# The first load of a decode kernel, issued as 16 rows and then 112

## The chip, the cores and the metric

The kernel runs on one core of a Trainium2 chip. The metric is the device time of one execution in microseconds; lower is better. The core's engines are TensorE (PE, whose weight loads are shown as PEld), VectorE (DVE), ScalarE (ACT), GpSimd (POOL) and SyncE (SP), which here issues nearly all transfers. Transfers run on 16 DMA engines beside them.

## The reference

One token is decoded. The input x (1 x 1 x 512) is layer-normalised; an attention block with 32 heads of 128 reads a cache of 8192 keys and values for each head; a gated linear unit makes a gate; the result is x + s · silu(g). All numbers are float32.

```python
xn = _layernorm(x, axis=-1)
# attention: q = (xn @ wq) in 32 heads of 128
scores = jnp.einsum("bhqd,bhkd->bhqk", q, k_cache) * (Dh ** -0.5)
p = _softmax(scores, axis=-1)
o = jnp.einsum("bhqk,bhkd->bhqd", p, v_cache)
s = o.transpose(0, 2, 1, 3).reshape(B, Sq, H * Dh) @ wo
# gate
h = _sigmoid(xn @ w_gate) * (xn @ w_up)
g = _silu(h @ w_down)
out = x + s * g
```

The key and value caches are 128 MiB (134 MB) each; wq and wo are 8 MiB each, and w_gate, w_up and w_down about 2.7 MiB each. Every byte is read once.

## The kernel before, in words

SBUF holds three large buffers, `slots[0]` to `slots[2]`, each 64 KB in each of 128 partitions. Heads are worked in 16 pairs. The keys of a pair fill one of the slots 0 and 1 by turns (two heads, 64 partitions each, 128 positions of 128 floats in a partition), the values of a pair fill slot 2. VectorE multiplies the keys with the query in place (L415) and sums over the head's 128 numbers (L416); TensorE and ScalarE do the maximum, the powers and the product with the values. At the end wo is loaded into a free slot in nine pieces (L484) and multiplied by VectorE and TensorE together.

Before the first pair the slots serve the small weights. wq lies in slot 2 as four blocks of 4096 columns (partition p holds rows 4p to 4p + 3 of wq) and is loaded in two halves, blocks 0 and 1 and then blocks 2 and 3; both are called by `load_queries` (L191). w_gate and w_up go to slot 0, the first pair's keys to slot 1. All of these go out on SyncE's queue, in the program's order: the first half of wq (L194) ahead of the branch into the compiled part (L196, where the engines meet), and the rest behind it. Only the input row x is loaded on ScalarE's queue (L240). w_down follows in slot 2, as a body of 128 rows and a remainder of 32 rows that go to every fourth partition (L321 and L324).

`load` (L163) is the helper behind every such transfer: it takes a name, gives that name a semaphore when it is new, adds 16 to the count to be waited for, issues the transfer and returns semaphore and count. A transfer that is waited for has landed when its semaphore has reached the count. VectorE waits for the first half of wq in the loop at L294 and starts `in_place` (L286), which scales wq's blocks by the normalised x (L289) and adds them up (L290, L307).

From the second pair on SyncE issues each load when its slot is free again: a key slot when VectorE has summed it, the value slot when TensorE has used it. A load therefore stands in the queue well before its turn on the DMA engines comes.

Of the kernel before, what the change touches and what calls it, by code (L numbers as in the profile page):

```python
# [13 lines left out]
P = 128  # L14
# [37 lines left out]
def kernel(  # L52
# [44 lines left out]
    DVE, ACT, SP, POOL = nc.vector, nc.scalar, nc.sync, nc.gpsimd  # L97
# [49 lines left out]
    def semaphore(name):  # L147
        return unused.pop(0)
# [14 lines left out]
    def load(eng, name, dst, src, *after):  # L163
        wait(eng, *after)
        if name not in loads:
            loads[name] = [semaphore(f"s_{name}"), 0]
        loads[name][1] += 16
        ins = eng.dma_start(dst, src)  # L168
        if not tc.compiled:
            tc.no_tile_sem_insts.add(ins.ins.name)  # L170
        ins.then_inc(loads[name][0], 16)
        return loads[name][0], loads[name][1]

    def wait(eng, *steps):
        for s in steps:
            if s is not None:
                eng.wait_ge(*s)
# [10 lines left out]
    xv = x.rearrange("a b d -> (a b d)")  # L188
    wq_t = slots[2].rearrange("p (k c) -> p k c", k=KT)
    wq_v = wq.rearrange("(p k) c -> p k c", k=KT)  # L190
    def load_queries(n):  # L191
        return load(SP, f"wq{n}", wq_t[:, n:n + 2, :], wq_v[:, n:n + 2, :])

    ld_wq = [load_queries(0)]  # L194
    tc.close()
    tc.compile()  # L196
    ld_wq.append(load_queries(2))
    wg_t, wu_t = (slots[0][:, n * KT * F:(n + 1) * KT * F].rearrange("p (k f) -> p k f", f=F) for n in range(2))
    ld_g = load(SP, "wg", wg_t, w_gate.rearrange("(p k) f -> p k f", k=KT))
# [157 lines left out]
    n = FL // NG  # L357
# [149 lines left out]
    for k, r in enumerate(W_DVE):  # L507
        n = k % 2
# [90 lines left out]
```

## Time and profile before

| | |
|---|---|
| median of three runs | 684.52 us (684.47 to 685.29) |
| the profiled execution | 684.89 us |
| its span, first to last instruction | 683.4 us |
| VectorE busy | 615.2 us (90%) |
| TensorE matmuls busy | 216.2 us (32%) |
| ScalarE busy | 44.6 us (7%) |
| mean granted TensorE clock | 0.668 |
| bytes read | 293.67 MB |

The page of a profile gives busy times of each engine over the span, then the span cut into 40 equal slices: a digit is the busy share in tenths, and a row of GB/s says what the DMA engines moved. Instructions are grouped by line, engine and operation, `out<-in` with the program's names for tensors and slots; "SPq" is the sequencer of SyncE, which issues transfers. A stretch of the run, given by its start and end in microseconds from the span's start, can be asked for by itself. For a transfer the page gives its size and the time from issue to landing. A packet counts with all its bytes at its start in such tables, so the GB/s of a stretch of a microsecond or two are rough.

### The profile page before, as it was taken

The numbers are of one execution on the slowest core, as the hardware profiler recorded it, in microseconds if no ns is written. First come the engines' busy times: TensorE is split into PE (matmuls) and PEld (weight loads), VectorE is DVE, ScalarE is ACT, GpSimd is POOL, SyncE is SP. The second block draws the span as 40 slices with busy tenths as digits, with TensorE's granted clock in tenths as the row PEclk, the third lists the DMA queues.
The fourth block names the chain that finished last, engine by engine and source line by source line (L and its number), as shares of the span: only waits on it lengthen the run. The fifth ranks groups of instructions, "written<-read, shape, count | busy, mean of one in ns | idle before, by whom it ended". The sixth has DMA issues, their size and how long they took to land. (4 is left out here: it accounts for less than half of the span.)

```text
span 683.4 us, 3400 instructions
## 1 busy us (share of the span) xinstructions
PE 216.2 (32%) x1376; PEld 62.0 (9%) x1376; DVE 615.2 (90%) x156; ACT 44.6 (7%) x142; POOL 2.6 (0%) x11
## 2 busy tenths in 40 slices
PE   0353024060513206050412406050422406060666
PEld 0120001010100101010100101010100101010110
DVE  3879999999999998998989899898989999999917
ACT  2130010000000101000000100000010101000010
POOL 0000000000000000000000000000000000000000
PEclk9996657575665757575665757575665757575886
DMA  9999999999999999999999999999999999999998
GB/s 382 429 440 472 430 430 430 430 430 430 430 430 430 430 430 430 430 456 456 437 430 430 430 430 430 430 430 430 430 430 445 449 441 399 476 399 430 430 430 337
DMA packets 7552, 293.67 MB, mean 430 GB/s; under 512 B 856, under 2 KB 864, under 8 KB 1664
## 3 DMA queue, kind: packets, MB, share of 16 engines
q1 hardware_dynamic: 7544, 293.67, 99.5%
q10 hardware_dynamic: 8, 0.00, 0.0%
HBM read 293.67 MB, written 0.00 MB: 430 GB/s over the span
## 5 line engine op out<-in xcount | busy, mean ns | idle before, releaser
L415 DVE TENSOR_TENSOR slot<-slot,q_all 128x16384 f32<-128x16384 f32 (+3 forms) x19 | 275.9, 14522 | 21.4 <-DMA slot<-in_A_k_cache_dram 21.4
L416 DVE TENSOR_REDUCE sc<-slot 128x128 f32<-128x16384 f32 (+3 forms) x19 | 276.0, 14525 | 0.7
L38 PE MATMUL psum<-slot,zeros 128*8 128x512 f32 x1024 | 145.5, 727 | 261.5 <-PEq L38 261.5
L38 PEld LDWEIGHTS psum<-slot,zeros 128*8 128x8 f32 x1024 | 30.2, 102 | 363.3 <-issue 363.3
L38 PE MATMUL psum<-ident,mx 128*1 128x128 f32 x32 | 8.7, 372 | 108.6 <-PEq L38 108.6
L437 ACT COPY o<-psum 128x512 f32<-128x512 f32 x16 | 9.4, 586 | 405.1 <-PE psum L38 405.1
L38 PE MATMUL psum<-slot,ones 128*128 (+3 forms) x36 | 15.9, 612 | 21.9 <-PEq L38 16.2
L290 DVE SCALAR_TENSOR_TENSOR slot<-slot,xn 128x1376 f32<-128x1376 f32 (+1 forms) x8 | 18.9, 2360 | 3.0 <-DMA slot<-in_A_wq_dram 2.7
L38 PE MATMUL psum<-o,pick 128*2 128x128 f32 x128 | 16.5, 272 | 12.8 <-PEq L38 12.8
L423 DVE STREAM_TRANSPOSE psum<-psum 32x128 f32<-32x128 f32 x16 | 5.0, 310 | 11.1 <-PE psum L38 11.1
L430 ACT ACTIVATE zeros<-sc,nb 64x128 f32<-64x128 f32 x32 | 12.8, 399 | 0.9
L38 PEld LDWEIGHTS psum<-o,pick 128*2 128x2 f32 x128 | 9.9, 84 | 29.6 <-issue 27.2
L428 ACT ACTIVATE nb<-psum 128x2 f32<-128x2 f32 x16 | 2.8, 172 | 150.9 <-PE psum L38 150.9
L38 PE MATMUL psum<-slot,o_all 128*1 128x128 f32 (+1 forms) x54 | 10.7, 510 | 5.3 <-DMA slot<-in_A_wo_dram 5.3
L38 PEld LDWEIGHTS psum<-ident,mx 128*1 128x1 f32 x32 | 1.9, 80 | 112.6 <-issue 112.6
L408 DVE TENSOR_REDUCE mx<-psum 1x2 f32<-1x128 f32 x16 | 4.4, 277 | 7.8 <-PE psum L38 7.8
L38 PE MATMUL psum<-zeros,rs 128*32 128x2 f32 x32 | 3.8, 188 | 23.5 <-PEq L38 23.5
L38 PE MATMUL psum<-mx,ones 1*128 1x2 f32 x32 | 8.4, 330 | 7.4 <-PEq L38 7.4
L515 DVE SCALAR_TENSOR_TENSOR q_all<-slot,o_all,q_all 128x512 f32<-128x512 f32 x15 | 10.0, 747 | 0.0
L38 PE MATMUL psum<-slot,o 128*1 128x512 f32 x26 | 5.5, 910 | 12.8 <-DMA slot<-in_B_w_down_dram 12.8
L38 PEld LDWEIGHTS psum<-slot,ones 128*128 128x128 f32 (+1 forms) x36 | 6.4, 201 | 31.3 <-issue 23.3
L38 PEld LDWEIGHTS psum<-mx,ones 1*128 1x128 f32 x32 | 7.5, 290 | 14.3 <-issue 14.3
(54 smaller groups left out, 60.5 us busy)
## 6 DMA issues: line engine op xcount, KB each, us to landing
slot<-in_A_k_cache_dram SPq DMA_DIRECT2D x2, 6144.0 KB, 37.9
slot<-in_A_v_cache_dram SPq DMA_DIRECT2D x3, 4096.0 KB, 22.7
slot<-in_A_wq_dram SPq DMA_DIRECT2D x2, 4096.0 KB, 16.3
slot<-in_A_k_cache_dram SPq DMA_DIRECT2D x2, 4096.0 KB, 40.5
slot<-in_A_k_cache_dram SPq DMA_DIRECT2D x2, 2048.0 KB, 42.4
slot<-in_B_w_gate_dram SPq DMA_DIRECT2D x1, 2752.0 KB, 26.7
slot<-in_B_w_up_dram SPq DMA_DIRECT2D x1, 2752.0 KB, 32.7
slot<-in_B_w_down_dram SPq DMA_DIRECT2D x1, 2560.0 KB, 24.1
```

The source lines that it names most:

```text
L38: ins = getattr(self.engine, name)(*args, **kwargs)
L290: return dve(DVE.scalar_tensor_tensor(y, w[:, k, cols], xn[:, k:k + 1], y, op0=ALU.mult, op1=ALU.add))
L408: DVE.reduce_max(mx[:1, 1:3], pt[0:1, :].rearrange("o (e p) -> o e p", e=2), axis=AX.X).then_inc(reduced, 1)
L415: wait(DVE, dve(DVE.tensor_mul(k[:, j, :], k[:, j, :], qb[:, i:i + 1, :].to_broadcast([P, n, Dh]))))
L416: summed[i] = dve(DVE.reduce_sum(sc[i % 2][:, j], k[:, j, :], axis=AX.X))
L423: turned_out[i] = dve(DVE.transpose(o, pn.rearrange("e (a r) -> e a r", r=WR)))
L428: wait(ACT, act(ACT.mul(nb, pm[:, :2], -SCALE)))
L430: ACT.activation(weights[h, :, e * HT:(e + 1) * HT], sc[i % 2][h].rearrange("p (g b) -> p g b", b=HT), AF.Exp, bias=nb[h, e:e + 1], scale= ...
L437: ACT.copy(o1, po).then_inc(copied, 1)
L515: ins = DVE.scalar_tensor_tensor(part[n], wo_t[:, r, :], col, part[n], op0=ALU.mult, op1=ALU.add)
```

## The change

`load_queries` takes partitions at which the load is cut, and issues one transfer for each run of partitions between cuts. The first half of wq is cut at partition 16: a transfer of 16 rows and one of 112 rows, each row 32 KB. Both have the same name, so they share one semaphore, and the count that is returned, and waited for by VectorE, is that of both. The second half is called without cuts and stays one transfer of 128 rows.

```diff
     wq_v = wq.rearrange("(p k) c -> p k c", k=KT)
-    def load_queries(n):
-        return load(SP, f"wq{n}", wq_t[:, n:n + 2, :], wq_v[:, n:n + 2, :])
-
-    ld_wq = [load_queries(0)]
+    def load_queries(n, *cuts):
+        for a, b in zip((0,) + cuts, cuts + (P,)):
+            ld = load(SP, f"wq{n}", wq_t[a:b, n:n + 2, :], wq_v[a:b, n:n + 2, :])
+        return ld
+
+    ld_wq = [load_queries(0, 16)]
     tc.close()
     tc.compile()
     ld_wq.append(load_queries(2))
```

## The prediction, made before the changed kernel was run

> **What bounds the kernel now.** I read the two strips of the page first, the 40 slices of DMA and of bandwidth, because a kernel that reads 293.67 MB once each should be judged by its stream of transfers.
>
> ```profile
> DMA  9999999999999999999999999999999999999998
> GB/s 382 429 440 472 430 430 430 430 430 430 430 430 430 430 430 430 430 456 456 437 430 430 430 430 430 430 430 430 430 430 445 449 441 399 476 399 430 430 430 337
> DMA packets 7552, 293.67 MB, mean 430 GB/s; under 512 B 856, under 2 KB 864, under 8 KB 1664
> q1 hardware_dynamic: 7544, 293.67, 99.5%
> ```
>
> The DMA engines are busy in every slice. Queue q1, SyncE's, holds 99.5% of sixteen engines' whole span, and only the first slice (382) and the last (337) fall clearly below 430 GB/s. To see how the ends differ from the middle I asked for four stretches of the run (columns: the stretch, its length, busy time and count of PE, PEld, DVE, ACT, POOL, the granted clock, DMA share, GB/s):
>
> ```profile
> 0.00:1.70 1.70, 0.00 (x0) 0.00 (x0) 0.00 (x0) 0.00 (x0) 0.21 (x4) 1.00 0.00 0
> 1.70:4.00 2.30, 0.00 (x0) 0.00 (x0) 0.17 (x1) 0.29 (x1) 0.97 (x6) 1.00 1.30 456
> 4.00:680.00 676.00, 215.27 (x1356) 61.62 (x1360) 614.48 (x153) 44.29 (x142) 1.38 (x1) 0.66 1.00 433
> 680.00:683.40 3.40, 0.97 (x24) 0.36 (x24) 0.58 (x2) 0.00 (x0) 0.00 (x0) 0.97 0.02 8
> ```
>
> Nothing moves before 1.70 us, the share is 1.00 for 676 us, and then there are 3.4 us of tail. So the time is start plus bytes over rate plus tail: whatever moves the start of the stream moves the end by as much, and whatever leaves engines at half speed for a moment is never made up, since no engine has a gap to catch up in. The chain of waits ends in the same stream:
>
> ```profile
> by line: DMA slot<-in_A_wo_dram 4.2%; PE psum L38 1.0%; SPq L168 0.4%; SPq L227 0.1%; issue 0.1%; DVE g_row L537 0.0%; DVE g_row L539 0.0%
> 650.71 28.58 DMA slot<-in_A_wo_dram
> ...
> 680.59 0.44 PE psum L38 x8
> ```
>
> The last transfer waited for is one of wo, landed shortly before 680.59; behind it come two small VectorE operations and the store.
>
> **The change part by part.** SyncE issues the first load in two pieces instead of one; the two add up to the same 4096 KB. The rows below are the first of SyncE's program, up to the branch into the body; slot is slot2 for the queries' weights, slots 0 and 1 for the gate, up and key loads. Before:
>
> ```order
> L594 UNCONDITIONAL_BRANCH
> L168 DMA slot<-in_A_wq_dram 128x8192
> L196 UNCONDITIONAL_BRANCH
> L168 DMA slot<-in_A_wq_dram 128x8192
> L168 DMA slot<-in_B_w_gate_dram 128x5504
> ```
>
> And with the change, at the same place of the same engine:
>
> ```order
> L596 UNCONDITIONAL_BRANCH
> L168 DMA slot<-in_A_wq_dram 16x8192
> L168 DMA slot<-in_A_wq_dram 112x8192
> L198 UNCONDITIONAL_BRANCH
> L168 DMA slot<-in_A_wq_dram 128x8192
> ```
>
> One 128-row issue became 16 and 112; all behind it, on this engine and on the four others, stands as it stood. These rows, of the DMA issues (size of one, median time to landing), of SyncE's timeline (start, length) and of its waits, price the issue and the start:
>
> ```profile
> slot<-in_A_wq_dram SPq DMA_DIRECT2D x2, 4096.0 KB, 16.3
> ...
> 0.74 0.38 SPq L168 DMA_DIRECT2D slot<-in_A_wq_dram  x1
> 1.91 0.33 SPq L168 DMA_DIRECT2D slot<-in_A_wq_dram  x1
> 36.85 0.33 SPq L168 DMA_DIRECT2D slot<-in_B_w_down_dram  x1
> 38.29 0.57 SPq L168 DMA_DIRECT2D slot<-in_B_w_down_dram  x1
> SPq L196 <- PEq L196: 0.4, 2, 0.3
> ```
>
> *The added issue.* It costs SyncE 0.33 to 0.57 us. SyncE waits for PE at L196 anyway, 0.3 us in its longest wait, so the start of the other engines and the second load slip by 0 to 0.3 us (0.57 − 0.3). That is hidden twice. In the queues, by the first load: 4096 KB at 430 GB/s are 9.8 us, and the second load is issued 1.2 us behind the first (1.91 − 0.74). On VectorE, by these rows:
>
> ```profile
> 12.53 0.23 DVE L279 TENSOR_SCALAR xn<-xc,st 128x4 f32<-128x4 f32 x1
> 12.90 2.35 DVE L289 TENSOR_SCALAR slot<-slot,xn 128x4096 f32<-128x4096 f32 x1
> 15.29 4.49 DVE L290 SCALAR_TENSOR_TENSOR slot<-slot,xn 128x4096 f32<-128x4096 f32 x1
> 22.50 4.49 DVE L290 SCALAR_TENSOR_TENSOR slot<-slot,xn 128x4096 f32<-128x4096 f32 x1 [2.73 <-DMA slot<-in_A_wq_dram]
> ```
>
> Its work on wq begins at 12.90 and then idles 2.73 us for the second load. A start 0.3 us late is swallowed there. If that cover were gone, the price is the same 0.3 us, and still not on the end, because the stream doesn't wait for VectorE in those microseconds. Sum: 0.
>
> *The semaphore.* Both pieces raise the first load's semaphore, and VectorE waits for twice the count, so it still starts when all 128 rows are in. One more 4-byte packet for each engine, 16 beside 7552: 0.
>
> *The start of the stream.* This is the term that can be a gain. From the stretch 4 to 680, the rate is 433 GB/s, at which 293.67 MB take 678.2 us. They ended just before 680.59, so at full rate they would have started at about 2.3 us, 1.6 us after the issue at 0.74 (the rate's last digit is worth 0.8 us). A first piece with an eighth of the rows can win no more than those 1.6 us, and nothing if the delay doesn't hang on the rows. The row nearest to it says that fewer rows aren't quicker: w_down's 32-row remainder took 0.57 us to issue and its 128-row body 0.33. That is the issue, not the first byte, so a little may remain; I take an eighth of the bound, 0.2 us, and keep 0 to 1.6.
>
> *Which engine writes where.* In place of one load in which every engine has eight rows, each engine now has one row of partitions 0 to 15 and then seven of the others. A row of 8192 floats is 32 KB, and at a sixteenth of 430 GB/s it takes 1.22 us: a row-time below. Eight row-times for each engine before, 1 + 7 after, if rows run at full speed wherever they land. No load of the trace goes to 16 neighbouring partitions. The nearest is w_down's remainder, 32 rows in every fourth partition:
>
> ```profile
> slot<-in_B_w_down_dram SPq DMA_DIRECT2D x1, 2560.0 KB, 24.1
> slot<-in_B_w_down_dram SPq DMA_DIRECT2D x1, 192.0 KB, 23.1
> ```
>
> The body landed at 36.85 + 24.1 = 60.95, the remainder at 38.29 + 23.1 = 61.39: 0.44 us for 192 KB, which at 430 GB/s take 0.46. So a quarter of the partitions is written at the full rate, and I take 0 for this term. But those rows lie four apart, and 16 rows side by side can fare worse: bounds 0 and +12.2 us, worked out under the first rival.
>
> [...]
>
> **Sum.** The profiled execution took 684.89 us, span 683.4 and 1.49 around it; −0.2 gives 684.7. The median of the three runs is 684.52, 0.37 below the profiled one, and I forecast against it: **684.3 us**.
>
> **The rivals.** *Neighbours share a way in: slower.* If four neighbouring partitions are written through one path no faster than one engine, the 16-row piece keeps four paths busy for four row-times while the others wait: +3 row-times, 3.7 us. Then come sevens of consecutive rows for each engine, whose neighbours' rows share groups of four; at worst two engines meet all the time, and seven row-times become 14. Together 4 + 14 = 18 against 8, +10 row-times or 12.2 us; midway, 7 row-times, +8.5 us. Nothing is caught up afterwards, as the share is 1.00 to the end. It decides as soon as two engines want one group. 684.5 + 8.5 = **693.0**, from 688.2 to 696.7. For it: an engine's and a path's rates can't be told apart while each engine has partitions of its own. Against it: the remainder's 0.44 us. [...]
>
> *The 16 rows don't go one to each engine.* No view names the engine of a packet. If four engines took four rows each and the 112 rows still went seven to each, those four would have 11 rows: +3 row-times, 3.7 us, **688.2**. If the 112 rows evened that out, nothing changes, and it falls to the forecast.
>
> *The start wins all it can: faster.* −1.6 us, **682.9**, if the whole delay to the first bytes hangs on the number of rows. Against it: the 32-row issue that was no shorter.
>
> **How the numbers follow.** The forecast, no contention and a start between 0 and 1.6 us earlier, most of it within 0.2%: 0.51. Shared paths: 0.40, so high because the one row that speaks of it touches every group once. Uneven spread: 0.06. The full gain: 0.03. Two tenths of a per cent, 1.37 us, is about what a measurement of this kernel can tell from no change. So faster 0.03, same 0.51, slower 0.46 (0.40 + 0.06). The forecast's own range is 683.5 to 685.3. The range given must take in most of the shared paths: below 683.5 I leave out the full gain, 0.03, and above 694.0 the upper third of the first rival, 0.13. Range **683.5 to 694.0**.
>
> **What would show it.** If I am right, the slice strip begins as before, the stretch 1.70 to 4.00 holds some 450 GB/s or more, the last wo transfer lands within half a microsecond of 680.5, and VectorE's first operation on wq starts at about 12.9. If paths are shared, the stretch from 2 to 7 us shows a DMA share near 1 at far less than 430 GB/s (a packet in hand counts as busy), the first wq operation starts some 5 to 8 us late, and the last transfer lands later by the same 4 to 12 us with the middle of the run unchanged. If the spread is uneven, some engines go idle or run ahead and the share falls below 1. If the 16-row issue is longer than 0.57 us, the added-issue term is wrong. What would overturn all of it is a change in the middle: a lower rate from 20 to 680 us, which nothing in this edit explains.

## The result, and the profile after

The changed kernel took **694.77 us** (median of four runs, 694.35 to 695.01) against 684.84 us for the kernel before on the same chip: a ratio of 1.0141, with a 95% interval of 1.0129 to 1.0153. That is 9.9 us slower, where 684.3 us were forecast; the range ended at 694.0. Of the cases that the prediction named, the first rival came true and not the forecast.

The strips and the DMA queue of the page after:

```profile
DMA  9999999999999999999999999999999999999997
GB/s 212 381 458 413 468 423 431 423 423 454 446 427 427 423 431 469 423 431 423 423 450 450 427 427 423 427 469 427 427 427 433 429 448 407 460 420 423 421 420 312
DMA packets 7568, 293.67 MB, mean 423 GB/s; under 512 B 872, under 2 KB 880, under 8 KB 1680
q1 hardware_dynamic: 7560, 293.67, 99.3%
```

The DMA row still reads 9 everywhere, as before. Only the row below it tells the loss: 212 GB/s in the first slice, where 382 stood, then 381 in the second, where 429 stood. "Busy" counts an engine that holds a packet, however slowly the packet moves: in the stretch from 6 to 18 us below the share is still 0.90 at 235 GB/s, and in the eight blocks further down 1.02 at 119. The 16 packets more (7568 against 7552) are all under 512 B (872 against 856) and go with the added load: three loads added make 48 more (7600), seven 112 (7664).

Three stretches of the kernel before (columns as in the prediction; the last two are DMA share and GB/s):

```profile
6.00:18.00 12.00, 1.17 (x4) 1.00 (x4) 6.73 (x10) 1.42 (x2) 0.00 (x0) 1.00 0.99 429
6.00:34.00 28.00, 6.96 (x14) 3.65 (x15) 19.93 (x21) 4.18 (x10) 0.00 (x0) 1.00 1.00 433
60.00:640.00 580.00, 170.78 (x1164) 48.47 (x1164) 549.31 (x82) 29.91 (x107) 0.00 (x0) 0.63 1.00 434
```

and two of the same of the kernel after:

```profile
6.00:18.00 12.00, 1.18 (x4) 1.01 (x4) 1.66 (x8) 1.85 (x4) 0.00 (x0) 1.00 0.90 235
...
60.00:640.00 580.00, 168.37 (x1132) 47.49 (x1132) 551.05 (x94) 29.91 (x107) 0.00 (x0) 0.63 1.00 434
```

From 60 to 640 us nothing has changed, 434 GB/s in both. From 6 to 18 us the first half of wq comes in at 235 GB/s in place of 429. What was lost there stays lost, because the share is 1.00 from 60 to 640 us. The timeline of VectorE shows the loss arriving at its first work on wq, and the chain of waits shows it at the end:

```profile
16.44 0.23 DVE L281 TENSOR_SCALAR xn<-xc,st 128x4 f32<-128x4 f32 x1
22.63 2.35 DVE L291 TENSOR_SCALAR slot<-slot,xn 128x4096 f32<-128x4096 f32 x1 [5.96 <-DMA slot<-in_A_wq_dram]
```

```profile
660.02 30.02 DMA slot<-in_A_wo_dram
...
690.71 0.44 PE psum L38 x8
```

The first operation on wq starts at 22.63 instead of 12.90, 9.7 us late. The last wo transfer is used at 690.71 instead of 680.59, 10.1 us late. Nearly the whole of the loss is made in the first 22 us.

The kept traces also hold the start and the length of every packet, though no view lists them; one packet is one row of 32 KB of wq. The last of the first 128 rows ends at 21.56 us instead of 12.48, 9.1 us late. In the kernel before, the first 16 rows take 1.75 us on average and the others 1.22, 16 of them under way at a time. In the kernel after, the first 16 take 3.68 us and the 112 others 2.12, again 16 at a time.

### The profile page after: what moved, and what is told of

Same layout as the page of the kernel before. It is cut to its first block, busy times and chain, and to the rows that moved or that the text cites. A ratio compares the mean times of both kernels' runs of the same rounds, so it can differ in the third digit from the quotient of the medians.

```text
span 693.5 us, 3401 instructions
## 1 busy us (share of the span) xinstructions
PE 221.6 (32%) x1376; PEld 62.6 (9%) x1376; DVE 615.8 (89%) x156; ACT 44.6 (6%) x142; POOL 2.6 (0%) x11
## 2 busy tenths in 40 slices
DMA packets 7568, 293.67 MB, mean 423 GB/s; under 512 B 872, under 2 KB 880, under 8 KB 1680
## 5 line engine op out<-in xcount | busy, mean ns | idle before, releaser
L38 PE MATMUL psum<-slot,zeros 128*8 128x512 f32 x1024 | 149.8, 745 | 252.0 <-PEq L38 252.0
L38 PE MATMUL psum<-slot,ones 128*128 (+3 forms) x36 | 17.4, 657 | 27.4 <-PEq L38 22.0
L291 DVE TENSOR_SCALAR slot<-slot,xn 128x1376 f32<-128x1376 f32 (+1 forms) x3 | 4.8, 1595 | 6.0 <-DMA slot<-in_A_wq_dram 6.0
```

The lines of the kernel that those rows point to most:

```text
L38: ins = getattr(self.engine, name)(*args, **kwargs)
L291: return dve(DVE.tensor_scalar(y, y, xn[:, 0:1], None, op0=ALU.mult))
```

## The experiments

Each time below is of one execution, but for the second run of the cut in the middle (two) and the even and odd partitions (ten). The theory was by now the prediction's first rival: neighbouring partitions share a way into the memory that is no faster than one DMA engine. Its own rivals were the cold start of the stream, the dividing itself (more pieces, fewer rows in each), and the source side, where 16 engines read rows that lie side by side. All edits are made to the changed kernel, and all but the pair on source and destination take slices of partitions:

```diff
-    def load_queries(n, *cuts):
-        for a, b in zip((0,) + cuts, cuts + (P,)):
-            ld = load(SP, f"wq{n}", wq_t[a:b, n:n + 2, :], wq_v[a:b, n:n + 2, :])
+    def load_queries(n, *parts):
+        for s in parts or (slice(0, P),):
+            ld = load(SP, f"wq{n}", wq_t[s, n:n + 2, :], wq_v[s, n:n + 2, :])
         return ld
```

The stretch from 6 to 18 us lies within the first half of wq wherever that is slow.

**The second half divided instead of the first.**

```diff
-    ld_wq = [load_queries(0, 16)]
+    ld_wq = [load_queries(0)]
-    ld_wq.append(load_queries(2))
+    ld_wq.append(load_queries(2, slice(0, 16), slice(16, P)))
```

> The first half of wq is one load of 128 rows again; the second half is cut at partition 16 instead, when the stream already runs. If rows of neighbouring partitions share a way into the memory, the place in the program is of no matter: about +10 us again, near 694.8. If the cost is one of the stream's cold start (the first bytes asked for by 16 small shares), it goes away: near 684.8.

694.45 us beside 684.95 of the kernel before. Its stretches:

```profile
6.00:12.00 6.00, 1.17 (x4) 1.00 (x4) 1.27 (x6) 1.28 (x2) 0.00 (x0) 1.00 1.02 432
14.00:28.00 14.00, 0.00 (x0) 0.00 (x0) 6.84 (x2) 0.00 (x0) 0.00 (x0) 1.00 0.92 225
```

The first half now flows at 432 GB/s and the second, with the stream long running, at 225. The cold start is out.

**Four loads of 32 rows: every fourth partition, or blocks.**

```diff
-    ld_wq = [load_queries(0, 16)]
+    ld_wq = [load_queries(0, *[slice(j, P, 4) for j in range(4)])]
```

> The first half of wq as four loads of 32 rows, each of every fourth partition. If neighbours share a way in, and the rows of w_down's remainder show the general case, each piece touches every group of four partitions once: 0 to +0.5 us, near 685. If dividing a load costs by itself, by the number of pieces or because each has few rows, four pieces cost at least what two did: 694.8 or more.

```diff
-    ld_wq = [load_queries(0, 16)]
+    ld_wq = [load_queries(0, *[slice(32 * j, 32 * j + 32) for j in range(4)])]
```

> The same four loads of 32 rows, but of 32 neighbouring partitions each. Shared ways in: each piece reaches half of the ways at most, so at least 8 row-times of 1.22 us more, +9.8 us or near 694.6; if the engines take the rows in such an order that only four ways are used at a time, +24 row-times, 29 us, near 714. Dividing a load costs by itself: the same time as the four loads of every fourth partition.

685.33 us and 694.80 us, beside 684.95. Both have four pieces of 1024 KB in the same place of the queue; only the partitions differ. The stretch from 6 to 18 us, every fourth partition first:

```profile
6.00:18.00 12.00, 1.18 (x4) 1.01 (x4) 5.26 (x10) 3.61 (x7) 0.00 (x0) 1.00 1.02 437
```

and the blocks:

```profile
6.00:18.00 12.00, 1.17 (x4) 1.00 (x4) 1.67 (x8) 2.96 (x7) 0.00 (x0) 1.00 1.06 219
```

Four pieces cost nothing that one execution can tell, and four pieces of the same size run at half the rate. Dividing is not the cost; which rows a piece holds is. All 16 engines work in both cases: the packets show 16 rows under way at a time, and behind the first 16 rows each takes 1.21 to 1.24 us in the first case and 2.32 to 2.58 in the second.

**The cut in the middle.**

```diff
-    ld_wq = [load_queries(0, 16)]
+    ld_wq = [load_queries(0, slice(0, 64), slice(64, P))]
```

> The first half of wq cut at partition 64, two equal pieces. Shared ways in: each piece reaches half of the ways, 16 row-times in place of 8, +9.8 us, near 694.6 (up to +29 us if only four ways are in use at a time). If it is the small first piece or the seven rows of an engine that cost, two pieces of four rows for each engine cost nothing: near 684.8.

> The cut at partition 64 once more. Its first run took 776.13 us, but only its start fits the shared ways (the rows of the two pieces took some 2.56 us); every later row of that execution was 12% slower as well. If that belonged to the execution and not to the cut, the time is now +9.8 us, near 694.6. If the cut at 64 leaves the engines out of step for good, it is near 776 again.

The first run took 776.13 us beside 684.95, the second, on another chip, 695.02 beside 685.24 (ratio 1.0143, 1.0114 to 1.0172). The first run's stretches:

```profile
6.00:18.00 12.00, 1.17 (x4) 1.00 (x4) 1.66 (x8) 2.41 (x7) 0.00 (x0) 1.00 1.05 219
60.00:640.00 580.00, 144.85 (x979) 40.53 (x978) 489.68 (x80) 26.12 (x93) 0.00 (x0) 0.61 1.00 386
```

and the second's:

```profile
6.00:18.00 12.00, 1.17 (x4) 1.00 (x4) 1.66 (x8) 2.40 (x7) 0.00 (x0) 1.00 1.06 219
...
60.00:640.00 580.00, 166.84 (x1132) 47.41 (x1132) 549.49 (x93) 29.89 (x107) 0.00 (x0) 0.63 1.00 433
```

The divided load is the same in both, 219 GB/s; the 776 us came from a stream that ran at 386 GB/s for the rest of that execution, which the same kernel didn't repeat on the other chip. Why that execution was slow stays open; the kernel before and the other edits ran at their usual speed on the first chip. Two pieces of 64 rows, with no 16-row piece and no sevens, cost as much as the change did.

**Source or destination.** The four loads once more, with pairs of slices, the partitions of the destination and the rows of the source:

```diff
-    ld_wq = [load_queries(0, 16)]
+    ld_wq = [load_queries(0, *[(slice(j, P, 4), slice(32 * j, 32 * j + 32)) for j in range(4)])]
```

> Changes what is computed: four loads of 32 rows, each from 32 rows side by side in the source, written to every fourth partition, so wq's rows stand in the wrong order. If the place in the on-chip memory decides, no cost: near 685. If it is the source, 32 neighbouring rows read by 16 engines at once, the cost of the blocks stays: near 694.8.

The reverse exchanges the two slices.

> The reverse, which also puts wq's rows in the wrong order: every fourth row of the source, written to 32 neighbouring partitions. If the on-chip side decides: near 694.8 as with the four blocks. If the source side decides: near 685.

685.16 us and 694.84 us, beside 685.24. From blocks to every fourth partition:

```profile
6.00:18.00 12.00, 1.17 (x4) 1.00 (x4) 5.00 (x10) 3.61 (x7) 0.00 (x0) 1.00 1.02 437
```

and from every fourth row to blocks of partitions:

```profile
6.00:18.00 12.00, 1.17 (x4) 1.00 (x4) 1.66 (x8) 2.98 (x7) 0.00 (x0) 1.00 1.06 219
```

The rate goes with the destination, whatever the source. The source side is out.

**Eight loads of 16 rows: every eighth partition, or blocks.** Here every engine has one row of each piece, so the order in which an engine takes its rows plays no part (the packets fit this: 16 rows are under way at a time).

```diff
-    ld_wq = [load_queries(0, 16)]
+    ld_wq = [load_queries(0, *[slice(j, P, 8) for j in range(8)])]
```

> Eight loads of 16 rows, each of every eighth partition, so that no two rows of a piece lie in one group of four neighbours and every engine has one row of a piece. If four neighbours alone share a way: 0 to +1 us, near 685. [...] If 16 rows in a load are dear whatever their places: eight times the +3 row-times of the first piece, +24 row-times, near 714.

```diff
-    ld_wq = [load_queries(0, 16)]
+    ld_wq = [load_queries(0, *[slice(16 * j, 16 * j + 16) for j in range(8)])]
```

> Eight loads of 16 neighbouring partitions, one row for each engine in each. [...] If the first piece of the changed kernel was only slow because it stood at the start, seven more such pieces cost far less each.

695.22 us beside 685.24, and 710.48 us beside 684.77: +10.0 and +25.7. Every eighth partition:

```profile
6.00:18.00 12.00, 0.59 (x2) 0.50 (x2) 1.37 (x7) 3.34 (x6) 0.96 (x6) 1.00 1.05 219
```

and the blocks, over a stretch long enough for rows that take several microseconds:

```profile
6.00:34.00 28.00, 1.17 (x4) 1.00 (x4) 1.66 (x8) 3.60 (x7) 0.43 (x3) 1.00 1.02 119
```

Half the rate, and a little over a quarter. That fits four engines to a way for 16 rows side by side, as assumed: 25.7 us over eight pieces are 3.2 us for one, where the prediction had 3.7. In the packets a row of these blocks takes 4.45 us behind the first piece. And rows eight apart, of which no two share a group of four neighbours, ran at 219 GB/s, half of the 437 of every fourth partition, as if two engines met on each way; by this theory, then, a way serves more than four neighbours. Which partitions share a way was not tested one by one.

**The large piece first.**

```diff
-    ld_wq = [load_queries(0, 16)]
+    ld_wq = [load_queries(0, slice(0, 112), slice(112, P))]
```

> The changed kernel's two pieces in the other order of size: 112 rows first, then the last 16. Shared ways: the last 16 rows cost +3 row-times as the first did, and the 112 rows of seven to an engine cost what is left, so +6 to +10 us, 691 to 695. If the 112 rows cost nothing by themselves and were only slowed behind the 16: +3.7 us, near 688.7.

693.72 us beside 684.77: +9.0, within the bounds for the shared ways and 5 us above the other. The 112 rows by themselves are slow, before any 16:

```profile
6.00:18.00 12.00, 1.18 (x4) 1.01 (x4) 1.67 (x8) 1.86 (x4) 0.00 (x0) 1.00 1.03 235
```

**Two pieces, even and odd partitions.**

```diff
-    ld_wq = [load_queries(0, 16)]
+    ld_wq = [load_queries(0, slice(0, P, 2), slice(1, P, 2))]
```

> Two loads again, but of the even and of the odd partitions, 64 rows each, so that each piece reaches every way equally. If sharing of ways is the whole cost, dividing in two costs nothing: 684.8 to 685.4. If dividing costs beside it, or such rows are taken in an order in which two engines meet, +9.8 us.

685.53 us (median of ten runs) against 684.77 (of thirteen): a ratio of 1.0009, 0.9999 to 1.0018, no difference that the runs can tell. The stretch from 6 to 18 us:

```profile
6.00:18.00 12.00, 1.18 (x4) 1.00 (x4) 6.35 (x10) 2.39 (x7) 0.00 (x0) 1.00 1.01 437
```

By that interval a load divided in this way costs at most 1.2 us, and no division that was run was clearly faster than the load in one piece.

## Why the prediction was wrong, point by point

- **What bounds the kernel: right.** The stream of transfers sets the end, and a loss at its start reached the end undiminished: 9.7 us at VectorE's first work on wq, 10.1 at the last transfer, 9.9 in the time.
- **The added issue: right in its cost, 0, but the slip was larger.** The issue of 16 rows took 0.40 us and that of 112 as much, where 128 rows had taken 0.38:

```profile
0.74 0.40 SPq L168 DMA_DIRECT2D slot<-in_A_wq_dram  x1
1.20 0.40 SPq L168 DMA_DIRECT2D slot<-in_A_wq_dram  x1
2.66 0.17 DVE L241 MEMSET x_row<- 128x128 f32 x1 [2.66 <-PEq L198]
SPq L198 <- PEq L198: 0.4, 2, 0.3
```

  VectorE's first operation started at 2.66 instead of 2.18, 0.48 us late, where 0 to 0.3 had been worked out: SyncE's wait of 0.3 us at the branch is there after the change as before, so it was no slack that the added issue could use. The slip was hidden all the same, since VectorE then waited 5.96 us for the load.

- **The start of the stream: the 0.2 us did not come.** After the change as before, no packet starts before 1.74 us, and the first ones do within the next 0.36. Before:

```profile
0.00:1.74 1.74, 0.00 (x0) 0.00 (x0) 0.00 (x0) 0.00 (x0) 0.21 (x4) 1.00 0.00 0
1.74:2.10 0.36, 0.00 (x0) 0.00 (x0) 0.00 (x0) 0.00 (x0) 0.12 (x1) 1.00 4.11 1183
```

and after:

```profile
0.00:1.74 1.74, 0.00 (x0) 0.00 (x0) 0.00 (x0) 0.00 (x0) 0.21 (x4) 1.00 0.00 0
1.74:2.10 0.36, 0.00 (x0) 0.00 (x0) 0.00 (x0) 0.00 (x0) 0.00 (x0) 1.00 5.28 728
```

  Each packet counts with its whole size when it starts, hence GB/s above what can flow; in the 0.36 us fewer packets start after (728) than before (1183), so eight times fewer rows bought no earlier start. The packets put the first one at 1.75 us before and 1.77 after.
- **"Which engine writes where": the step that failed.** The prediction took 0 for this term because w_down's 32-row remainder was written at full rate. That row was read rightly and proved the wrong thing. Its 32 rows lie in every fourth partition, and the run with every fourth partition shows that this is the very choice that is free (437 GB/s), while 32 rows in a block run at 219. The text noted that this row touched every group once and that 16 rows side by side could fare worse, and yet made it the reason for the value 0, and so for the forecast. In place of 0 the term measured 8.2 us for the mean engine, by the packets, and with it the first rival was the case that came.
- **The first rival: right in kind, low by 1.4 us.** It gave +8.5; 9.9 was measured. Half way between its bounds of 3 and 10 row-times lie 6.5, or 7.9 us, and not the 7 that it took. Its path for four neighbours alone was too narrow, since rows eight apart, which share no such group, cost 10.0 us.
  - The 16-row piece was 3.7 in its sum. In the middle of a stream it measures 3.2 (an eighth of the 25.7). In the changed kernel it lost less, 1.9 us, because the first 16 rows are slow even undivided (3.68 us on average instead of 1.75).
  - The 112 rows were 4.8 in its sum and measured 6.3: seven rows for each engine, 14.8 us instead of 8.5, within the bounds of 0 to 8.5.
  - The engines no longer finish together, so the last row is 9.1 us late where the mean is 8.4 (the first rows also start 0.15 us later). The rest, up to the 9.9, isn't traced.
  - The rival's sevens were consecutive rows for each engine, which was the author's assumption. With consecutive rows the first of the four loads of every fourth partition would start at partitions 0, 8, 16 and so on, the very set that ran at half the rate (219 GB/s) in the eight loads; it ran at 437 GB/s. So the engines seem to take their rows in another order, which no run here shows, and that the 7 row-times came near is luck.
- **The range** ended at 694.0, because the upper third of this rival was left out; the time lay there, 0.8 us above it.
- **Uneven spread, and the full gain:** neither showed. The sign that the prediction named for an uneven spread, engines that go idle or run ahead and a share below 1, is not there behind the load: the share is 1.00 from 24 to 40 us and from 60 to 640 us. The 16 rows of the first piece started within 0.8 us and the 17th row only when the first of them had ended, which fits one row for each of 16 engines.

## What to carry to other kernels

Not the dividing cost here, but which partitions a piece held. Pieces of every second or every fourth partition were written at 437 GB/s and all 128 in one piece at 429, but blocks of 32 or 64, and every eighth partition, at 219, and blocks of 16 at 119. Of the divisions that were run, only those into every second or fourth partition cost nothing that the runs can tell. When a stream of transfers is the bound, judge it by GB/s and not by the busy share, and ask of a row that is brought as evidence whether it could have come out otherwise under the rival.

## What was not expected of the hardware

Under the theory of shared ways a row takes two or four times as long where two or four engines meet on a way; little came on top of that. In the packets a row takes 1.21 us in an undivided load, at most 2.60 in the pieces that ran at half the rate (2.1 times as long at the median, 2.54 to 2.57) and 4.45 in blocks of 16 (3.7 times). That the last is less than four times may come from pieces that overlap, as the 16 rows of a piece start up to 1.9 us apart there; the rate of a single way can therefore not be read off.

One execution ran at 386 GB/s from 60 to 640 us where the others had about 433, and its divided load was still at 219, so what slowed it was not these ways.

The start of a first load hung on its shape and not simply on its size. For blocks of 16, 32, 112 and all 128 partitions the issue took about 0.4 us and the first packet started at 1.75 to 1.77 us. For blocks of 64 and for every second, fourth or eighth partition the issue took 0.57 to 0.64 us and the first packet started at 2.10 to 2.15. In the stretch from 1.74 to 2.10 us every second and every fourth partition show 91 GB/s each, where the undivided load shows 1183.
